# Turning k one slot sooner and q one slot later, and merging the last-key products of a duo, in a fused attention and MLP kernel

## The chip, the cores and the metric

The kernel runs on one core of a Trainium2 chip. The metric is the device time of one execution in microseconds; less is better. A time is the span of the profile plus about 1.8 us (535.75 against 534.0 for the profiled execution of the kernel before).

## The reference

```python
# q, k, v: (8, 8, 576, 64); tau = 0.02
scores = (q @ k.T) / 8
thresh = max(scores, -1) - tau
scores = where(scores >= thresh, scores, -1e9)
attn   = softmax(scores)
x      = (attn @ v)  -> (4608, 512)        # heads side by side
h      = x @ w_in                          # 512 x 2048
out    = (h - tanh(h)) @ w_out             # 2048 x 512
```

## The kernel before

The work is cut into 32 pairs of heads. A pair has nine query tiles of 128 rows, counted j = 0 to 8: four of the first head, one in the middle that holds the 64 rows left over of both heads, four of the second head. The program is a row of slots, one per tile. In a slot TensorE makes the scores of one tile, one step of the MLP of an earlier batch, and the value products of an older tile; a batch of four pairs has 32 MLP steps in 36 slots, so four slots have none. Two neighbouring tiles form a duo, whose ten blocks of transposed weights lie in one tile `pT`; the ninth key block of both tiles (64 keys each) shares one block.

```python
# attend(i): value product of a duo
for ab in range(2):
    blocks = [(4 * ab + ab + c, c) for c in range(4)]
    blocks.append((4, 4 + ab))               # the shared block of weights
    for n, (blk, c) in enumerate(blocks):
        nc.tensor.matmul(out=po[:, (j - 1 - 5 * hh) + ab, :],
            lhsT=pt[:, blk * P : (blk + 1) * P], rhs=vb[:, hh, c, :],
            start=(n == 0), stop=(n == 4))
```

Before a pair's scores, its k and q are split into high and low halves by GpSimd (`split`) and turned (`turn`): by nine TensorE transposes into one of the two big PSUM buffers `ps_big`, which the scores use as well, and a VectorE copy to `kT` or `qT`. GpSimd then copies `kT` to `kS` with the halves swapped. From pair 9, odd pairs' q, and pair 30's, is turned by a transposing transfer instead, which the sync engine's queue issues.

```python
def q_by_dma(p):
    return p >= 2 * HPAIR and (p % 2 == 1 or p == 30)
# ... cut ...
PREP = (
    # ... loads cut ...
    (8, lambda p: split(p, "k")), (7, lambda p: split(p, "q")),
    (5, lambda p: turn(p, "k")), (4, split_v),
)
for p in range(1, NPAIR):
    first = TPP * p - AHEAD                  # slot of the pair's first scores
    for d, f in PREP[3 if p == 1 else 0 :]:
        d -= p == 1 and d in (3, 5)
        plan.setdefault(first - d, []).append(lambda p=p, f=f: f(p))
    d = 5 if q_by_dma(p) else 3 - (p == 1)
    plan.setdefault(first - d, []).append(lambda p=p: turn(p, "q"))
```

## Time and profile before

| | us |
|---|---|
| median of the runs before the change | 537.72 |
| lowest and highest of them | 537.52, 538.24 |
| the profiled run | 535.75 |
| TensorE busy, of a span of 534.0 | 512.9 |
| VectorE, ScalarE, GpSimd busy | 427.2, 438.2, 290.0 |

### The profile page before, as it was taken

The page shows a single profiled execution, that of the slowest core. Times are in us where ns is not written, and L with a number is a line of the kernel's source. Part 1 is how long each engine was busy: PE and PEld are TensorE (multiplying, and loading weights), DVE is VectorE, ACT ScalarE, POOL GpSimd, SP SyncE. Part 2 cuts the span into 40 slices and gives each one's busy share as a digit, 9 for nine tenths or more (in the row PEclk, how much of TensorE's full clock was granted, in tenths as well). Part 3 has the DMA queues.
Part 4 walks back from the last instruction along what each step waited for, and adds up shares of the span by engine and source line. Part 5 has one row for each costly group of instructions (what it writes and reads, how often), then busy time and mean ns, then how long its engine had stood idle before and what let it go on. Part 6 is the DMA issues. An engine that isn't in the chain of part 4 may idle for free.

```text
span 534.0 us, 13042 instructions
## 1 busy us (share of the span) xinstructions
PE 512.9 (96%) x4782; PEld 287.9 (54%) x4782; DVE 427.2 (80%) x1202; ACT 438.2 (82%) x630; POOL 290.0 (54%) x390
## 2 busy tenths in 40 slices
PE   8989899999999999999999999999999999999997
PEld 4666565555555555555555555555555455444444
DVE  5889877989888988889888988898888888554440
ACT  5999888999898989899888989898989989543330
POOL 7999995767555666657555755566665720000000
PEclk9999999999999999999999999999999999999999
DMA  7555656999998888798988999899989985401113
GB/s 209 178 186 147 207 164 146 184 199 181 178 183 178 180 187 196 169 183 188 190 186 183 191 183 185 171 176 196 189 168 187 193 153 107 105 21 39 39 41 79
DMA packets 204768, 85.76 MB, mean 161 GB/s; under 512 B 172320, under 2 KB 197152, under 8 KB 204704
## 3 DMA queue, kind: packets, MB, share of 16 engines
q1 hardware_dynamic: 204112, 84.51, 74.2%
q8 instruction: 37, 0.61, 0.5%
q10 hardware_dynamic: 592, 0.43, 0.3%
q14 instruction: 27, 0.22, 0.1%
HBM read 36.70 MB, written 9.44 MB: 86 GB/s over the span
## 4 chain that ended last, share of the span: by engine, by line
PE 69%; DVE 15%; POOL 7%; ACT 3%; issue 2%; DMA 2%; SPq 0%; DVEq 0%; POOLq 0%; ACTq 0%
PE psY L521 21%; PE psH L495 18%; PE psS L327 14%; DVE sc L337 7%; PE psO L440 5%; DVE g L514 3%; PE psS L317 3%; PE psHt L495 3%; PE ps_k L241 2%; POOL kS L270 2%; DVE kT L264 2%; ACT pT L403 1%; ACT z L374 1%; DVE yo L534 1%; POOL w_in_sb L628 1%
## 5 line engine op out<-in xcount | busy, mean ns | idle before, releaser
L337 DVE TENSOR_SCALAR_CACHE_REDUCE sc<-psS 128x576 f32<-128x576 f32 x288 | 216.1, 752 | 22.4 <-PE psS L327 13.8
L374 ACT ACTIVATE z<-sc,nb 128x576 bf16<-128x576 f32 x256 | 193.4, 768 | 19.7 <-DVE nb L354 19.7
L521 PE MATMUL psY<-w_out_sb,g 128*128 128x512 bf16 (+1 forms) x592 | 146.0, 374 | 0.8 <-DVE yo L534 0.8
L270 POOL COPY kS<-kT 64x1152 f16<-64x1152 f16 x62 | 70.7, 1141 | 127.3 <-DVE nb L354 125.6
L411 ACT ACTIVATE pT<-zT 128x1152 f16<-128x1152 bf16 (+1 forms) x130 | 138.9, 1068 | 0.4 <-DMA zT<-z 0.4
L495 PE MATMUL psH<-xT,w_in_sb 128*128 128x512 bf16 x480 | 124.0, 379 | 2.3 <-DVE g L514 2.3
L327 PE MATMUL psS<-kT,qT 128*128 128x512 f16 (+1 forms) x512 | 104.4, 285 | 6.0 <-DVE sc L337 4.3
L508 ACT ACTIVATE th<-psH 128x512 f32<-128x512 f32 x128 | 75.4, 589 | 36.0 <-PE psH L495 34.8
L327 PEld LDWEIGHTS <-qT 128*128 128x128 f16 x1024 | 72.3, 97 | 55.7 <-issue 8.7
L327 PE MATMUL psS<-kS,qT 128*128 128x512 f16 x496 | 101.3, 286 | 0.8 <-POOL kS L270 0.7
L514 DVE SCALAR_TENSOR_TENSOR g<-th,psH 128x512 bf16<-128x512 f32 x128 | 87.3, 682 | 17.5 <-ACT th L508 17.5
L521 PEld LDWEIGHTS <-g 128*128 128x128 bf16 x592 | 50.7, 98 | 56.9 <-issue 4.0
L495 PEld LDWEIGHTS <-w_in_sb 128*128 128x128 bf16 x576 | 49.2, 98 | 58.2 <-issue 4.5
L440 PEld LDWEIGHTS <-pT 128*128 128x128 f16 x1280 | 55.7, 98 | 25.2 <-issue 1.9
L440 PE MATMUL psO<-vb,pT 128*128 128x65 bf16 x1280 | 61.2, 193 | 0.0
L194 POOL TENSOR_TENSOR khl<-kraw,khl 128x576 f16<-128x576 f32 x31 | 39.7, 1279 | 2.6
L194 POOL TENSOR_TENSOR qhl<-qraw,qhl 128x576 f16<-128x576 f32 x31 | 39.7, 1279 | 2.6
L403 ACT ACTIVATE pT<-psZ 128x640 f16<-128x640 bf16 (+1 forms) x54 | 35.4, 658 | 5.8 <-PE psZ L394 5.4
L264 DVE COPY kT<-ps_k 128x1152 f16<-128x1152 f16 x31 | 23.4, 756 | 14.1 <-PE ps_k L241 14.0
L534 DVE COPY yo<-psY 128x512 f32<-128x512 f32 (+1 forms) x31 | 21.1, 682 | 13.1 <-PE psY L521 11.1
L455 DVE TENSOR_TENSOR osb<-psO,rc 128x256 bf16<-128x256 f32 x64 | 27.2, 424 | 2.2
L354 DVE TENSOR_SCALAR nb<-mx 128x6 f32<-128x6 f32 (+1 forms) x160 | 24.5, 153 | 2.3
(81 smaller groups left out, 508.2 us busy)
## 6 DMA issues: line engine op xcount, KB each, us to landing
vraw<-in_v_dram SPq DMA_DIRECT2D x32, 256.0 KB, 3.8
out_dram<-yo SPq DMA_DIRECT2D x32, 256.0 KB, 2.9
kraw<-in_k_dram SPq DMA_DIRECT2D x31, 256.0 KB, 3.2
qraw<-in_q_dram SPq DMA_DIRECT2D x31, 256.0 KB, 3.7
wt<-in_moe_w_in_dram SPq DMA_DIRECT2D x8, 512.0 KB, 4.5
wt<-in_moe_w_out_dram SPq DMA_DIRECT2D x8, 512.0 KB, 4.5
zT<-z SPq DMA_TRANSPOSE x104, 3.5
kraw<-in_k_dram SPq DMA_DIRECT2D x32, 32.0 KB, 3.0
```

What stands on the lines that cost most here:

```text
L194: nc.gpsimd.tensor_tensor(out=hl[:, :, 1, :], in0=x, in1=hl[:, :, 0, :], op=ALU.subtract)
L270: nc.gpsimd.tensor_copy(out=o, in_=i)
L327: nc.tensor.matmul(out=ps[:, dst], lhsT=lhs, rhs=kk[:, src], start=(n == 0), stop=(n == 1),)
L337: nc.vector.tensor_scalar(out=sc, in0=ps[:, lo : lo + S], scalar1=SC, scalar2=None, op0=ALU.mult, op1=ALU.max, accum_out=mx[:, c : c + 1],)
L374: nc.scalar.activation(out=z, in_=sc, func=ACT.Prelu, bias=nb, scale=1.0, alpha=STEEP)
L403: nc.scalar.activation(out=pt[:, off * P : (off + n) * P], in_=ps[:, 0 : n * P], func=ACT.Exp)
L411: nc.scalar.activation(out=pt[:, 0 : n * P], in_=zts.pop(i)[:, 0:n, :], func=ACT.Exp)
L440: nc.tensor.matmul(out=po[:, (j - 1 - 5 * hh) + ab, :], lhsT=pt[:, blk * P : (blk + 1) * P], rhs=vb[:, hh, c, :], start=(n == 0), stop=(n ...
L495: nc.tensor.matmul(out=ps, lhsT=w_in_sb[:, c, n * P : (n + 1) * P], rhs=xs[m][:, c, :] if m < B else xR[:, c, :, :], start=(c == 0), stop= ...
L508: nc.scalar.activation(out=th, in_=ps, func=ACT.Tanh)
L514: nc.vector.scalar_tensor_tensor(out=gs[m][:, n, :], in0=th, scalar=-1.0, in1=ps, op0=ALU.mult, op1=ALU.add,)
L521: nc.tensor.matmul(out=ps, lhsT=gs[m][:, n, ms * P : (ms + 1) * P], rhs=w_out_sb[:, n, cols], start=(n == 0), stop=(n == DF_C - 1),)
```

## The change

Its intent: one matmul and one weight load less per duo, and turns placed where VectorE's copy does not hold up the reductions.

```diff
-        for ab in range(2):
-            blocks = [(4 * ab + ab + c, c) for c in range(4)]
-            blocks.append((4, 4 + ab))
-            ... ten products of 65 columns, start on the first of five
+        t = j - 1 - 5 * hh
+        nc.tensor.matmul(
+            out=po[:, t : t + 2, :], lhsT=pt[:, 4 * P : 5 * P],
+            rhs=vb[:, hh, 4:6, :], start=True, stop=False, skip_group_check=True,
+        )
+        for n in range(8):
+            ab, c = divmod(n, 4)
+            blk = 5 * ab + c
+            ... eight products of 65 columns, no start
@@
+            if d == 5 and p >= 5:
+                d = 6
@@
-        d = 5 if q_by_dma(p) else 3 - (p == 1)
+        d = 5 if q_by_dma(p) else (2) if p >= 5 else 3 - (p == 1)
```

More of the change, by code (lines that the diff above doesn't have):

```diff
@@ L434, in attend @@
         pt, hh = pts.pop(i), int(j > 4)
-        for ab in range(2):
-            blocks = [(4 * ab + ab + c, c) for c in range(4)]
-            blocks.append((4, 4 + ab))
-            for n, (blk, c) in enumerate(blocks):
-                nc.tensor.matmul(
-                    out=po[:, (j - 1 - 5 * hh) + ab, :],
-                    lhsT=pt[:, blk * P : (blk + 1) * P], rhs=vb[:, hh, c, :],
-                    start=(n == 0), stop=(n == 4),
-                )
+        t = j - 1 - 5 * hh
[6 more added lines that the diff above has]
+            blk = 5 * ab + c
+            nc.tensor.matmul(
+                out=po[:, t + ab, :], lhsT=pt[:, blk * P : (blk + 1) * P],
+                rhs=vb[:, hh, c, :], start=False, stop=(n == 7), skip_group_check=True,
+            )
     osb = {}
```

## The prediction

> **What bounds the kernel now.** I read the page's busy digits first, then the busy time of each engine in equal windows, then the list of waits, and last the order of time around each turn of k and q.
>
> ```profile
> PE   8989899999999999999999999999999999999997
> DVE  5889877989888988889888988898888888554440
> ACT  5999888999898989899888989898989989543330
> ```
>
> TensorE is at nine tenths or more nearly everywhere after the first 60 us; VectorE and ScalarE follow closely until slice 33. "Busy" is no proof for TensorE, because a matmul's record is longer than its turn in the pipe, so I looked at the windows (columns: window, its length, then busy us and count of PE, weight loads, VectorE, ScalarE, GpSimd; clock; DMA share; GB/s):
>
> ```profile
> 60.00:120.00 60.00, 54.56 (x591) 33.88 (x592) 51.62 (x152) 54.19 (x83) 46.14 (x59) 1.00 0.74 172
> 180.00:240.00 60.00, 59.31 (x568) 33.07 (x567) 53.28 (x153) 54.31 (x76) 36.35 (x48) 1.00 0.88 184
> ```
>
> and at the starts in the order of time (start us, us, engine, line, operation, count, wait if any):
>
> ```profile
> 250.91 0.48 PE L440 MATMUL psO<-vb,pT 128*128 128x65 bf16 x10
> 251.22 0.41 PE L327 MATMUL psS<-kT,qT 128*128 128x512 f16 x2
> ...
> 257.75 0.67 PE L241 MATMUL ps_k<-ident_f,khl 128*128 128x128 f16 x9
> 258.25 0.41 PE L327 MATMUL psS<-kT,qT 128*128 128x512 f16 x2
> ...
> 259.61 0.46 PE L429 MATMUL psO<-vb,pT 128*128 128x130 bf16 x5
> 259.90 0.41 PE L327 MATMUL psS<-kT,qT 128*128 128x512 f16 x2
> ```
>
> From start to start, ten value products of 65 columns take 0.31 us (31 ns each; a duo elsewhere takes 0.32), nine 128-column turns 0.50 us (56 ns each), five of 130 columns 0.29 us (58 ns each). The matmuls follow each other at the pace of their columns. In 120 to 420 us TensorE waits visibly for VectorE only 3.7 us in all (2.1 us for scores, 1.6 us for the hidden product); before that there is more. So the kernel is bound by TensorE's columns, and a reordering can win only its waits: little in the steady part, more between 55 and 120 us. The tail after 466 us holds no attention and cannot change.
>
> **What the Trainium skill says.** "TensorE: Matmul & The Clock Gate", section "Back-to-back issue gap", gives N/2.4 + 2.5 ns for a warm matmul: 29.6 ns for 65 columns, 55.8 for 128, 56.7 for 130. The trace agrees within 2 ns. The same section says that in a stream of weight load and matmul pairs 128 columns cost about 81 ns; the trace doesn't: every ps_k turn has its own load and comes 56 ns after the last. So a weight load is hidden here, and dropping one wins nothing by itself. The same page, "Architectural detail: the array is 16× 32×32, not 1× 128×128", says that VectorE's queue is strictly first in, first out. The trace agrees, as the 1.08 us below shows: a copy that waits for its turn holds up the reductions behind it. "PSUM — Partial Sum Buffer", the rule on accumulation, says that a first matmul clears the written bits of the whole bank, so that a second first in the same bank would spoil an open group. The new order has one first per duo, so nothing is spoilt; no run yet shows it.
>
> **The change, part by part.**
>
> *Value product.* There are 4 duos in each of 32 pairs of heads, 128 in all (1280 products of 65 columns now). Each changes from ten 65-column products to one of 130 and eight of 65. By the starts above: before 10 x 31.5 = 315 ns, after 58 + 8 x 31.5 = 310 ns. The columns stay; one matmul's fixed cost and a hidden load go. 128 x 5 ns = 0.6 us, all on TensorE's path. The first product now needs the late half of pT, but TensorE shows no wait for ScalarE at this line today, only 1.9 us of "issue".
>
> *k a slot sooner (27 pairs, from pair 5).* The nine turns move from behind the 64-column scores of the middle tile (L317) to before them. No work is added. What moves is the 0.76 us copy on VectorE:
>
> ```profile
> 229.00 1.04 PE L495 MATMUL psH<-xT,w_in_sb 128*128 128x512 bf16 x4
> 229.88 0.48 PE L440 MATMUL psO<-vb,pT 128*128 128x65 bf16 x10
> 230.20 0.67 PE L241 MATMUL ps_k<-ident_f,khl 128*128 128x128 f16 x9
> ...
> 230.97 0.76 DVE L264 COPY kT<-ps_k 128x1152 f16<-128x1152 f16 x1 [1.08 <-PE ps_k L241]
> ```
>
> VectorE stands 1.08 us at the copy because TensorE does a hidden product (0.87 us) and a duo (0.32 us) first. Over the run such waits are 14.0 us in 21 places. After the change the turn comes just behind the step of the slot before, which has no duo, so much of that idle time goes and the copy's 0.76 us is done before the scores of the next tile arrive. VectorE starts some 0.7 us less late. This is worth something only where lateness reaches TensorE: once in four pairs, where four slots have no MLP step:
>
> ```profile
> 236.97 0.41 PE L327 MATMUL psS<-kT,qT 128*128 128x512 f16 x2 [0.15 <-DVE sc L337]
> 237.21 0.41 PE L327 MATMUL psS<-kS,qT 128*128 128x512 f16 x2
> 237.84 0.41 PE L327 MATMUL psS<-kT,qT 128*128 128x512 f16 x2 [0.22 <-DVE sc L337]
> ```
>
> With the hidden pipe the two stalls are about 0.3 and 0.4 us of pitch. Most of it stays: the scores started at 235.36 end near 236.0, their reduction (0.75 us) began at 236.16, so VectorE can be at most 0.15 us earlier there, and the second reduction follows at once. I count 0.15 us for each of six such places (pairs 9, 13, ... 29): 0.9 us.
>
> *q a slot later (TensorE-turned pairs only).* In the steady part the score behind the q turn loses about 0.12 us in one pair of four; I let it go, 6 x 0.12 = 0.7 us. Between 60 and 92 us it costs more:
>
> ```profile
> 74.63 0.41 PE L327 MATMUL psS<-kT,qT 128*128 128x512 f16 x2 [0.44 <-DVE sc L337]
> 90.53 0.41 PE L327 MATMUL psS<-kT,qT 128*128 128x512 f16 x2 [0.83 <-DVE sc L337]
> ```
>
> There the q turn stands in the one slot in which VectorE has the normalisation of a half pair (0.19 + 0.42 + 0.34 us) as well. Moved on a slot it meets none. Half of 0.44 + 0.83 and of pair 5's 0.40 + 0.38 us around 60 to 61 us may go: 1.0 us.
>
> *What it costs.* In pairs 5 and 6 GpSimd is late with casts. Pair 6's low halves of k begin at 67.39 and take 1.28 us, to 68.67, while the middle scores start at 67.96: the sooner turn must wait some 0.7 us. Pair 5 has 57.48 (56.20 + 1.28) against 56.78: again 0.7 us. Part of that returns as waits that are then shorter; I take half of it, 0.7 us lost.
>
> Sum: 0.6 + 0.9 + 0.7 + 1.0 - 0.7 = 2.5 us. I round to 2.3 us for stalls I haven't seen: 537.7 - 2.3 = 535.4 us.
>
> **Rivals.** First, the weight load is the limit of the value product, and a ninth load less frees a whole pair's 31.5 ns: 128 x 31.5 = 4 us, giving about 533. For it speaks that the products alternate above 29.6 ns; against it the 56 ns turns with a load each and the unchanged column count. Second, the q copy becomes a new wait: it now has one slot until its first scores instead of two. In the steady part a slot is 1.6 us (58 us for 36 slots), and copy plus one reduction take 1.5 us, so that it just fits; if it misses by 0.3 us in each of the 14 pairs, 4 us come back, some 538 to 540 us. Third, the sooner k turn takes one of the two big score buffers before the middle scores, which then wait for the reduction of the tile before (ends 241.05 by 240.30 + 0.75, turn would end at 240.97): near nothing, or 0.2 us in 27 pairs, 5 us at worst. Fourth, everything moved was hidden anyway: only the 0.6 us remain, 537.1 us.
>
> **Range and chances.** The steady waits of TensorE and its early ones together are under ten us, 2% is 10.8 us. To be faster by 2% nearly every wait would have to go; to be slower by 2% each of 27 pairs would have to gain 0.4 us. Neither is likely. The range from 533.3 to 537.5 takes in the weight-load rival and the one in which all was hidden, but not new stalls in every pair.
>
> **What would show it.** Right: the 130-column product takes 58 ns to the next start, duos 310 ns; the wait of kT for ps_k falls well below 14 us; the waits at 74.6 and 90.5 us are gone or halved; 0.15 us less at pairs 9 to 29; TensorE's first wait for khl on GpSimd near 57 and 68 us. Wrong: a new wait of scores for the copy of qT in every even pair, a longer wait of the middle scores (L317) for the reductions, or duos of 285 ns.

## More of the kernel before

The profiled run is 2 us shorter than the median.

The waits of the whole run on transfers of q, which the prediction passed over, read (who waited, for what, us in total, times, longest; PEld is TensorE's weight load):

```profile
PEld L327 <- DMA qT<-qhl: 1.9, 4, 0.9
PE psS L327 <- DMA qT<-qhl: 0.4, 1, 0.4
```

## The result, and the profile after

The changed kernel takes 535.74 us (median of 4, 535.43 to 536.77) beside 537.73 us before. The ratio is 0.9965 with an interval of 0.9948 to 0.9982. Ratios here are the mean time of one kernel's fast runs over that of the other's of the same rounds, so they are not quite the ratio of the medians quoted. The result is correct, so the single start flag per duo spoils nothing here.

The busy row and one of the windows hardly differ, but for the DMA share of the window, 0.97 where it was 0.88; in the other windows it moves both ways (same columns as in the prediction):

```profile
PE   8989799999999999999999999999999899999997
```

```profile
180.00:240.00 60.00, 59.41 (x552) 33.47 (x551) 53.56 (x155) 54.62 (x76) 35.48 (x45) 1.00 0.97 184
```

*The value product.* In the order of time, one duo of the changed kernel (start, us, engine, line, operation):

```profile
250.16 0.22 PE L437 MATMUL psO<-vb,pT 128*128 128x130 bf16 x1
250.22 0.42 PE L444 MATMUL psO<-vb,pT 128*128 128x65 bf16 x8
250.47 0.41 PE L327 MATMUL psS<-kT,qT 128*128 128x512 f16 x2
```

From 250.16 to 250.47 the nine products take 0.31 us, within the display's rounding of the ten. Taken exactly from the starts of all 128 duos, the median is 313 ns against 317 ns; the 130-column product with its own load takes 57 ns.

*The turn of k.* It now stands in front of the middle scores (L317), and the copy follows at once:

```profile
226.92 1.03 PE L524 MATMUL psY<-w_out_sb,g 128*128 128x512 bf16 x4
227.78 0.67 PE L241 MATMUL ps_k<-ident_f,khl 128*128 128x128 f16 x9
228.38 0.44 PE L317 MATMUL psS<-kT,qT 128*64 128x512 f16 x4
```

```profile
228.55 0.76 DVE L264 COPY kT<-ps_k 128x1152 f16<-128x1152 f16 x1
229.23 0.15 DVE L354 TENSOR_SCALAR nb<-mx 128x6 f32<-128x6 f32 x1
229.29 0.75 DVE L337 TENSOR_SCALAR_CACHE_REDUCE sc<-psS 128x576 f32<-128x576 f32 x1
```

Before, the copy of the same pair started at 230.97 after 1.08 us of idling. VectorE's waits for ps_k fall from 14.0 us in 21 places to 6.8 us in 15. What it does for the stall that the prediction looked at:

```profile
236.35 0.41 PE L327 MATMUL psS<-kT,qT 128*128 128x512 f16 x2
236.59 0.41 PE L327 MATMUL psS<-kS,qT 128*128 128x512 f16 x2
237.22 0.41 PE L327 MATMUL psS<-kT,qT 128*128 128x512 f16 x2 [0.22 <-DVE sc L337]
```

The first wait (0.15 us before) is no longer listed; by the starts, TensorE lost 0.31 us there before (from one start to the next, beyond what the work between them takes elsewhere) and loses 0.22 us now. The second loss is unchanged at 0.38 us.

*Between 60 and 92 us.* The waits at 74.63 and 90.53 us are gone: the scores at 74.63 us list no wait, and the q turns of pairs 6 and 7, from their start to the scores behind them, take 0.67 and 0.50 us where they took 1.10 and 1.49 us. A part comes back one pair later: pair 8's takes 1.11 us where it took 0.54.

*GpSimd near 57 us.* This one came as predicted for pair 5:

```profile
57.82 0.68 PE L241 MATMUL ps_k<-ident_f,khl 128*128 128x128 f16 x9 [0.72 <-POOL khl L194]
```

*And what no step of the prediction names.* At pair 30, whose q comes by a transfer, the first scores wait:

```profile
420.54 1.03 PE L524 MATMUL psY<-w_out_sb,g 128*128 128x512 bf16 x4
423.11 0.42 PE L327 MATMUL psS<-kT,qT 128*128 128x512 f16 x2 [1.55 <-DMA qT<-qhl]
```

The trace of before has this wait too, but shorter:

```profile
423.42 0.42 PE L327 MATMUL psS<-kT,qT 128*128 128x512 f16 x2 [0.39 <-DMA qT<-qhl]
```

The transfer is not slow. Its data is ready long before, on GpSimd, but the sync queue issues it late. Before (GpSimd's last instruction on q, then the queue):

```profile
413.67 1.28 POOL L194 TENSOR_TENSOR qhl<-qraw,qhl 128x576 f16<-128x576 f32 x1
...
410.88 3.67 SPq L382 DMA_TRANSPOSE zT<-z  x2
...
417.40 1.52 SPq L382 DMA_TRANSPOSE zT<-z  x1
419.01 0.52 SPq L537 DMA_DIRECT2D out_dram<-yo  x1
419.65 1.31 SPq L253 DMA_TRANSPOSE qT<-qhl  x1
```

After:

```profile
410.45 1.28 POOL L194 TENSOR_TENSOR qhl<-qraw,qhl 128x576 f16<-128x576 f32 x1
...
409.58 4.97 SPq L382 DMA_TRANSPOSE zT<-z  x2
...
419.65 1.35 SPq L253 DMA_TRANSPOSE qT<-qhl  x1
```

GpSimd is 3.2 us sooner, and the queue issues at the same 419.65 us. In both traces it is busy without a pause before that: the second of the two zT issues shown ends at 414.55 us, and four loads, a zT and a store follow, each at most 0.12 us after the last. The changed kernel starts that second zT issue 1.35 us sooner (411.92 us against 413.27), but it takes 2.63 us instead of 1.28; why was not taken apart. TensorE ends the MLP step before pair 30 1.46 us sooner and waits 1.16 us longer. To see the account at a glance, here is the start of a pair's first scores in several traces, and the time from pair 4 to the last matmul. Start-up differs by up to 1.1 us between the traces (pair 4 starts at 51.84 to 52.92 us), which the last column leaves out (it is the fourth number less the first).

| trace (us) | pair 4 | pair 29 | pair 30 | last matmul | pair 4 to last |
|---|---|---|---|---|---|
| before | 52.00 | 409.78 | 423.42 | 529.97 | 477.97 |
| before, again | 51.84 | 410.62 | 424.12 | 530.67 | 478.83 |
| after | 52.25 | 408.43 | 423.11 | 529.62 | 477.37 |
| after, again | 52.20 | 408.36 | 423.28 | 529.78 | 477.58 |

So by the one trace of each, 1.35 us are won by pair 29 and 0.36 us remain at the end, while the medians differ by 2.0 us. The experiments had to explain both numbers.

### The profile page after: what moved, and what is told of

Its sections match the earlier page's. It is cut to its first block, busy times and chain, and to the rows that moved or that the text cites. A ratio compares the mean times of both kernels' runs of the same rounds, so it can differ in the third digit from the quotient of the medians.

```text
span 533.6 us, 12797 instructions
## 1 busy us (share of the span) xinstructions
PE 511.7 (96%) x4654; PEld 289.6 (54%) x4654; DVE 427.5 (80%) x1202; ACT 438.3 (82%) x630; POOL 291.0 (55%) x390
## 4 chain that ended last, share of the span: by engine, by line
PE 76%; DVE 8%; POOL 8%; DMA 2%; issue 2%; ACT 2%; SPq 0%; POOLq 0%; DVEq 0%; ACTq 0%
PE psY L524 23%; PE psH L498 19%; PE psS L327 16%; PE psO L444 4%; DVE sc L337 4%; PE psS L317 3%; PE psHt L498 3%; PE ps_k L241 2%; DMA kraw<-in_k_dram 2%; DVE g L517 2%; POOL kS L270 2%; PE psO L429 1%; POOL w_in_sb L631 1%; POOL khl L194 1%; PE ps_q L241 1%
## 5 line engine op out<-in xcount | busy, mean ns | idle before, releaser
L524 PE MATMUL psY<-w_out_sb,g 128*128 128x512 bf16 (+1 forms) x592 | 146.0, 374 | 0.8 <-DVE yo L537 0.8
L444 PE MATMUL psO<-vb,pT 128*128 128x65 bf16 x1024 | 53.3, 194 | 0.0
L444 PEld LDWEIGHTS <-pT 128*128 128x128 f16 x1024 | 44.3, 98 | 11.1
L437 PE MATMUL psO<-vb,pT 128*128 128x130 bf16 x128 | 28.2, 220 | 0.0
```

The lines of the kernel that those rows point to most:

```text
L444: nc.tensor.matmul(out=po[:, t + ab, :], lhsT=pt[:, blk * P : (blk + 1) * P], rhs=vb[:, hh, c, :], start=False, stop=(n == 7), skip_group_ ...
L524: nc.tensor.matmul(out=ps, lhsT=gs[m][:, n, ms * P : (ms + 1) * P], rhs=w_out_sb[:, n, cols], start=(n == 0), stop=(n == DF_C - 1),)
```

## The experiments

Twelve kernels ran, with five rounds each; all gave correct results. Within a call the runs of the kernel before are shared (medians 537.34, 537.00 and 537.87 us); the first two calls ran on one chip, the third on another. At the start theory A was the prediction's own: only stalls between engines count. Its rivals were that the trace of before was a lucky one (B), that the transfers take the gain back (C), and, for the product, that a load is worth a whole turn.

### before_again: the kernel before, unchanged

> The unchanged kernel, once more, for the noise of times and of traces. Theory A (the gain is the stalls that moved: about 1.7 us of it in the traces, from the product and the shorter waits): ratio 1.000 within 0.1%, and the new trace lies like the first one: start of the first score of pair 29 near 409.8 us, and of pair 30 near 423.4 us. Rival B (the trace of before caught a luckily short run, because it reads 535.75 us while the unprofiled runs read 537.5 to 538.2; the usual run has about 2 us more in waits for transfers): the new trace is 1 to 2.5 us longer, and the excess stands in waits on a transfer, most likely at pair 30's transposed q.

Measured: 536.83 us (536.40 to 537.20), ratio 0.9991 (0.9979 to 1.0004). The trace is 0.7 us longer than the first one at the end. Pair 29 starts at 410.62 us, not at 409.8. The excess stands in transfers, but not at pair 30, which waits only 0.24 us: the first scores of pair 27 wait 0.39 us for q, and there is this from ScalarE:

```profile
ACT pT L411 <- DMA zT<-z: 1.5, 2, 1.1
```

It was 0.4 us in one place in the first trace. That is B in kind, though less than B said (1 to 2.5 us, most likely at pair 30): the kernel before loses a varying amount to transfers, and the first trace was a good draw.

### after_again: the changed kernel, unchanged

> The changed kernel once more. Both theories: ratio 0.9965 within 0.15%. Theory A: pair 29 starts its scores again near 408.4 us, 1.35 us sooner than before; the 1.5 us wait of pair 30's first score for the transfer of its q comes and goes. Rival C (the transfer queue is the second bound, and takes back what TensorE wins): the wait at pair 30 is there again, between 1 and 2 us, and the tail starts only 0.3 to 0.5 us sooner than in the trace of before.

Measured: 535.56 us (534.94 to 535.64), ratio 0.9966 (0.9952 to 0.9979). Pair 29 starts at 408.36 us, and pair 30 waits 1.77 us. This is as C said, so the wait belongs to the changed kernel. (The last matmul starts 0.19 us sooner than in the first trace of before, a little less than C's 0.3.)

### product_only: only the merged value product

```diff
 the kernel before, with attend() of the changed kernel
```

> Only the value product of the change; k and q turn when they did. Theory A: 128 duos x 4 ns (317 ns before, 313 ns after, by the starts in the two traces) = 0.5 us, ratio 0.9990 (0.998 to 1.000). Rival (a dropped weight load is worth a whole 31 ns turn): 4 us, ratio 0.9926. Rival C: 0.5 us at pair 29, less at the end.

Measured: 535.56 us (535.49 to 535.72), ratio 0.9969 (0.9957 to 0.9982). Both expected ratios missed, and C's loss at the end too (0.52 us are still there at the last matmul, counted from pair 4). The product alone gives nearly the whole gain of the median, three times its direct 0.5 us. The trace does show the 0.5 us: pair 29 starts 0.51 us sooner when both are counted from pair 4 (357.27 us against 357.78). The duos are the same length as in the changed kernel. The rest must be in what the trace of before, a good draw, does not have.

### q30_by_pe: pair 30's q turned by TensorE

```diff
 changed kernel, and
-        return p >= 2 * HPAIR and (p % 2 == 1 or p == 30)
+        return p >= 2 * HPAIR and p % 2 == 1
```

> The changed kernel, but pair 30's q is turned by TensorE like that of the other even pairs and no transfer is needed for it. It adds nine turns of 56 ns, 0.5 us of TensorE, and one 0.75 us copy on VectorE. Theory A (the wait at pair 30 is a real stall of up to 1.5 us in the changed kernel): 0.5 to 1.0 us faster than after_again in the traces, and the tail starts 1 us sooner. Rival C (the transfers as a whole are late): the wait moves to the transposed zT of the same tiles and the time is that of after_again or 0.5 us longer.

Measured: 534.32 us (534.04 to 534.64), ratio 0.9946 (0.9933 to 0.9958). It is 1.24 us shorter than after_again, a little more than expected, in spite of nine turns more. The last matmul starts at 528.59 us instead of 529.78. The wait at pair 30 is therefore on the path to the end, and doesn't reappear elsewhere.

### before_sooner_transfer and before_sooner_transfer_2: the transfers of q one slot sooner, nothing else

```diff
 the kernel before, and
-        d = 5 if q_by_dma(p) else 3 - (p == 1)
+        d = 6 if q_by_dma(p) else 3 - (p == 1)
```

> The kernel before, with only the transposing transfers of q (13 pairs) issued one slot sooner; nothing on TensorE changes. Theory D (the kernel before loses 1 to 2 us in most runs because the transposed q of pairs 9, 11, 27 and 30 lands just when its first score wants it; the changed kernel's gain in the median is largely that this happens in fewer pairs): landings 1.0 us or more ahead of the first score in all 13 pairs, 1.2 to 1.8 us faster, ratio 0.9970 (0.9962 to 0.9980). Theory A (only TensorE's and VectorE's stalls count): ratio 0.9990 to 1.0005.

Measured: 536.02 us over the five fast runs (536.20 with the slow one), ratio 0.9983 (0.9971 to 0.9995), which just misses both D's range and A's. One run of six was slow (868.82 us at clock 0.558); the profile fell in it, so that there was no fast trace to read. Again:

> The same as before_sooner_transfer, whose one profile fell into a slow run at clock 0.558. Theory D: again ratio 0.998, and its trace shows no first score of a pair waiting for its q, and lies within 0.3 us of the first trace of before at pair 29 and 0.4 us under it at the end, so that the rest of the 1.6 us between that trace's run (535.75 us) and the usual 537.3 us has another cause, to be seen in the trace. Rival: the waits at pairs 9, 11, 27 or 30 are still there.

Measured: 535.93 us (535.54 to 536.48), ratio 0.9968 (0.9955 to 0.9980), so the two differ by what the noise allows. In the trace q lands at least 1.66 us before its first scores in all 13 pairs, and no wait for qT is left. So waits for q are worth between 0.9 and 1.7 us in the usual run of the kernel before. The expected place of pair 29 (within 0.3 us of the first trace) missed: it is 0.80 us later. It already was 0.43 us later at pair 4, and 0.63 us more are lost between pairs 9 and 10 (0.2 us come back at pair 11), where ScalarE waits for another transfer:

```profile
ACT pT L411 <- DMA zT<-z: 2.0, 3, 1.1
```

### after_sooner_transfer: the changed kernel with the same

```diff
 changed kernel, and
-        d = 5 if q_by_dma(p) else (2) if p >= 5 else 3 - (p == 1)
+        d = 6 if q_by_dma(p) else (2) if p >= 5 else 3 - (p == 1)
```

> The changed kernel with the transfers of q one slot sooner. Theory D: the wait of 1.5 to 1.8 us at pair 30 is gone or halved, 534.3 us, ratio 0.994 (0.9930 to 0.9955), as when TensorE turns pair 30's q. Theory A: 535.6 us, ratio 0.9966. If the transfer queue as such were the bound, the waits would turn up at zT, and the time be that of the changed kernel or worse.

Measured: 533.94 us (533.68 to 534.13), ratio 0.9941 (0.9930 to 0.9953), as theory D said. The place in question:

```profile
420.54 1.03 PE L524 MATMUL psY<-w_out_sb,g 128*128 128x512 bf16 x4
421.40 0.41 PE L327 MATMUL psS<-kT,qT 128*128 128x512 f16 x2
```

The first scores of pair 30 follow the MLP step after its own 0.86 us, with no wait; q landed at 419.48 us. From pair 4 to the last matmul the trace takes 475.64 us, against 477.37 us for the changed kernel.

### k_and_q: only the turns

```diff
 the kernel before, with the two plan lines of the changed kernel
```

> The two turns as in the change, the value product as before. Theory A: everything but the product's 0.5 us, so 1.2 us faster, ratio 0.9975. Theory D: in the trace six gains of about 0.2 us at pairs 9 to 29 less a loss of 0.2 to 0.9 us at pairs 4 and 5, a wait of 0.5 to 1.3 us at pair 30, ratio 0.997 to 1.000. If k and q were worth nothing, as product_only at 0.9969 beside 0.9966 for the whole change suggests, ratio 0.9990 to 1.0010.

Measured: 536.51 us (534.82 to 537.70), ratio 0.9987 (0.9971 to 1.0003). It lies in theory D's range, but A's 0.9975 lies inside its interval and the third theory's range (0.9990 to 1.0010) overlaps it, so the ratio decides nothing. The trace tells more: from pair 13 to pair 29 it takes 231.26 us against 231.89 in the kernel before, so 0.63 us are won there; then

```profile
424.73 0.42 PE L327 MATMUL psS<-kT,qT 128*128 128x512 f16 x2 [1.63 <-DMA qT<-qhl]
```

and from pair 4 to the end it is 0.39 us longer than the first trace of before (478.36 us).

### k_only: only k

```diff
 the kernel before, and
+            if d == 5 and p >= 5:
+                d = 6
```

> k a slot sooner from pair 5, q as before. Theory: loses 0.7 us near 57 us waiting for GpSimd's halves of k (0.9 us at the start of pair 5's scores by the trace of the changed kernel), part of it returned by pair 8; gains 0.09 us at each of pairs 13 to 29. Net between 0 and 0.5 us faster at pair 29, ratio 0.999 to 1.001. Rival (k alone carries the reordering): ratio 0.9975.

Measured: 536.16 us (535.54 to 537.63), ratio 0.9987 (0.9974 to 1.0001). From pair 4 to pair 29 it takes 357.52 us, 0.26 us less than before, as expected, including a 0.51 us wait for q at pair 11. It also corrects an attribution. The prediction gave 0.12 us per four pairs to the later q, for the score behind the q turn. In this kernel q turns where it always did, and:

```profile
246.59 0.67 PE L241 MATMUL ps_q<-ident_f,qhl 128*128 128x128 f16 x9
247.10 0.41 PE L327 MATMUL psS<-kT,qT 128*128 128x512 f16 x2
```

Nine turns take 0.51 us, so nothing is lost there any more (0.62 us before, from 245.92 to 246.54). It is so in all five such places between 120 and 365 us: 0.50 to 0.52 us here, 0.62 in the trace of before. The sooner k alone had removed it; that it did so by leaving VectorE less late fits, but was not shown.

### product_order_only: the new order without the merging

```diff
 product_only, but the first product of a duo split
-        nc.tensor.matmul(out=po[:, t : t + 2, :], lhsT=pt[:, 4 * P : 5 * P],
-            rhs=vb[:, hh, 4:6, :], start=True, ...)
+        for ab in range(2):
+            nc.tensor.matmul(out=po[:, t + ab, :], lhsT=pt[:, 4 * P : 5 * P],
+                rhs=vb[:, hh, 4 + ab, :], start=(ab == 0), ...)
```

> The kernel before with the new order of the value product (shared block of weights first, one first flag per duo), but with ten 65-column products: no matmul and no load is saved. Theory E (the 4 ns per duo that the merged product saves, and the transfers that then land in time by a little, make the gain of product_only): 317 ns per duo as before, ratio 0.9990 to 1.0005. Rival F (the order or the flags do it, not the merging): ratio 0.9970, as product_only.

Measured: 537.44 us (537.09 to 538.14), ratio 0.9997 (0.9984 to 1.0011). Its interval does not touch that of product_only (0.9957 to 0.9982). So it is the merging, not the order or the flags. Its trace has the waits on transfers again:

```profile
ACT pT L411 <- DMA zT<-z: 2.2, 2, 1.7
```

Together with the other traces this gives a pattern. The transfer of q takes, from issue to landing, 5.2 to 5.6 us at pair 11 in the five traces at the old transfer slot that have ten products per duo (before, before_again, k_only, k_and_q, product_order_only), and 5.3 to 5.8 us at pair 27. In the four with the merged product (product_only, after, after_again, q30_by_pe) it takes 4.2 to 4.6 and 3.8 to 4.1 us, and no first score waits there. Nor do these four list any wait of ScalarE for zT.

The traces say more about why. The page lists a DMA queue of kind "instruction" (packets, MB, share); it reads, before and after:

```profile
q8 instruction: 37, 0.61, 0.5%
q8 instruction: 36, 0.59, 0.5%
```

Every kernel with ten products per duo has 37 of these 16 KB packets, every one with nine has 36; it also has 128 matmuls and 128 weight loads less. The traces hold the time of each single packet. In the five traces with ten products one packet starts at 144.1 to 146.0 us, inside the transfer of pair 11's q, and one inside that of pair 27's. In the four it starts at 147.3 to 148.1 us, after pair 11's q has landed, and none falls in pair 27's. At pairs 17 and 19 it is the other way round: there the four have a packet in the transfer, which takes 4.3 to 4.7 us, and the five have none and take 3.2 to 3.9 us; but q lands in time in all nine. In 13 traces, the 47 transfers of q with such a packet starting inside them have a median of 4.5 us, the 121 without one 3.4 us. ScalarE's wait near 124 us follows the packet too (0.4 to 1.7 us, as a transfer of zT lands; in k_only and k_and_q the view puts it down to TensorE). It is there when the packet starts at 119.3 to 120.4 us, during that transfer or just before it, and absent when it starts at 123.9 to 124.7 us. One kernel with nine products, k_from_7_sooner_transfer below, has the packet at 120.4 us, and a wait of 1.1 us with it. So what counts seems to be when the packet comes, and the merging moves it. No run moved the packets alone, so this path is not shown by an experiment.

### product_sooner_transfer: the product and the sooner transfer, old turns

```diff
 product_only, and the transfer line of before_sooner_transfer
```

> The value product of the change and the sooner transfer of q; the turns of k and q on TensorE as before. By the traces the turns are worth 0.85 us at the start of pair 29 (1.35 for the whole change less 0.5 for the product) once no transfer takes it back. Theory: 534.8 us, 0.85 us longer than after_sooner_transfer's 533.94, ratio 0.9958. Rival (the turns of k and q are worth nothing, as 0.9969 beside 0.9966 says): 534.0 us, ratio 0.9941.

Measured: 535.49 us (535.30 to 535.75), ratio 0.9960 (0.9947 to 0.9972), as expected by the ratio. The microseconds are 0.7 above the expected ones, since the kernel before was 0.9 us slower. Against after_sooner_transfer's 0.9941, the turns of k and q are worth about 1 us (0.0019 of 537) when no transfer takes it back. The rival's 0.9941 lies just outside the interval; the two intervals overlap a little (0.9947 to 0.9953), so zero is unlikely rather than excluded by the times. From pair 4 to the last matmul the traces say 1.4 us (477.05 against 475.64).

### k_from_7_sooner_transfer: k sooner only where GpSimd is ready

```diff
 after_sooner_transfer, and
-            if d == 5 and p >= 5:
+            if d == 5 and p >= 7:
```

> The changed kernel with the sooner transfer, and k turned sooner only from pair 7: pairs 5 and 6 don't wait for GpSimd's halves. Theory: the 0.9 us lost at the start of pair 5's scores stays away, of which 0.6 us were already returned by pair 6; so 0.2 to 0.5 us faster than after_sooner_transfer, 533.5 us, ratio 0.9934. Rival (VectorE and ScalarE take back all of it by pair 8): 533.9 us, ratio 0.9941.

Measured: 533.67 us (533.01 to 533.79), ratio 0.9922 (0.9910 to 0.9935). It has the lowest ratio, below both expected ones. The comparison with after_sooner_transfer crosses two calls, in which the kernel before differs by 0.87 us, so its size is uncertain: 0.27 us by the medians, 1.0 us by the ratios. The traces, from pair 4 to the last matmul, differ by 0.26 us (475.38 against 475.64), as expected. They are 0.62 us apart from pair 9 to pair 30, and 0.37 us of that is lost again between pairs 30 and 31, where ScalarE has the longest of these waits:

```profile
ACT pT L411 <- DMA zT<-z: 3.3, 4, 1.3
```

## Why the prediction was right or wrong

The number was right: 535.7 us for 535.4 predicted, inside the range of 533.3 to 537.5 us. That it came so close is in part luck: the sum reached it partly by other terms than its own.

- **The value product, 0.6 us.** Right in mechanism and size: 4 ns per duo, 128 x 4 = 0.5 us. Left out was an indirect part of about 1.2 us: with the merged product the usual run loses less to the transfers of q and zT (product_only 0.9969, order alone 0.9997). That merging does it is shown; the path, by all traces the times of the "instruction" packets, is not tested by itself.
- **k in the steady part, 0.9 us.** The copy's wait fell by half, as said. The gain at the scores in the slots without an MLP step is 0.09 us a place, not 0.15, which fits VectorE's waits for scores (13.8 us before, 19.0 after): part of its lead may have gone into waiting for its input. There are five such places, not six: pair 9 has a single wait, 0.25 us in both traces. But the 0.12 us entered for q also comes from k, so that k wins about 0.21 us in each group of four pairs. Pairs 13 to 29, four such groups, are 0.71 us shorter in k_only (231.89 - 231.18), and 0.87 us shorter in the changed kernel beyond what the product wins there (231.89 - 230.80, less 231.89 - 231.67).
- **q in the steady part, 0.7 us.** This step failed in its attribution: k_only shows that k alone removes the stall behind the q turn. k_only and k_and_q have the same ratio, 0.9987. The places are five here too. Together the two terms were 1.6 us; from pair 9 to pair 29 the changed kernel wins 1.46 us by one trace of each, of which product_only has 0.51, so about 0.95 us are left for k and q.
- **The early part, 1.0 won and 0.7 lost.** The 0.72 us wait of pair 5 came. Pair 6's did not, since TensorE was by then later itself. From pair 4 to pair 9 the net gain is 0.14 us (67.70 us before, 67.56 after) for 0.3 predicted. k_from_7_sooner_transfer, in which k of pairs 5 and 6 turns when it did before, splits it: its 66.93 us are 0.77 us less than before, so the sooner k of these two pairs loses about 0.6 us. Both terms were a little smaller than predicted.
- **Rivals.** The load as the limit (4 us) is out: 313 ns per duo, where it needed 285. A wait for the copy of qT in even pairs did not appear in the steady part; VectorE now waits 7.3 us for ps_q, with no loss on TensorE that the traces show. The middle scores wait for a reduction once more than before, 0.35 us at pair 8. "Hidden anyway" comes nearest to the fate of the turns, but it was not hidden: it was won, and then lost at pair 30.
- **What was missing.** The step "bound by TensorE's columns, and a reordering can win only its waits" left the transfers out of the list of waits. The transfer of pair 30's q, issued at 419.65 us before and after, took back most of the 1.35 us, which q30_by_pe and after_sooner_transfer show by giving 1.2 and 1.7 us. And the median of before was not the trace of before: the 2 us between them were the hint, and by the two runs of before_sooner_transfer 0.9 to 1.7 us of such a gap are waits for q. The two errors nearly cancelled, which was luck.

## What to carry to other kernels

Compare the profiled run's time with the median before reading a trace: if they differ by as much as the gain you look for, the trace does not show what the gain will come from, and several traces are needed. When an engine is made faster, look at each transfer that lands just ahead of its reader, and ask when its queue issues it, not how long it takes: here data lay ready for 5 to 8 us behind other issues in the same queue, and moving the issue one slot was worth 0.5 to 1.7 us (by the ratios, according to what else was changed), about as much as the reordering of the turns. When a change alters how many instructions an engine has, look also at whether other transfers now meet different ones. Credit a part of a change only after it has run alone and with the waits that mask it taken away.

## What the Trainium skill lacked or had wrong

- "TensorE: Matmul & The Clock Gate", section "Back-to-back issue gap", gives about 81 ns per matmul of 128 columns in a stream of load and matmul pairs. Here nine such pairs take 0.50 to 0.51 us, 56 ns each; the 130-column product with its own load takes 57 ns, and two 65-column products with a load each become one for a saving of only 4 ns. The same section's formula for an isolated gap is what holds in the stream.
- "DMA: Bandwidth & Descriptors", section "Issuing engines are not separate DMA queues", calls the time to initiate a DMA on a sequencer "usually small relative to the DMA itself". Here, in the traces of before and after, a transposing issue of q occupies the sync queue for 1.3 to 2.3 us, of a time to landing of 3.3 to 5.4 us, and a finished q waited 4.7 us (before) and 7.9 us (after) from its last GpSimd instruction's end to its issue at pair 30.
- No page that I read says that a data transfer takes longer when a packet of the "instruction" queue falls inside it. Here the transfers of q with one have a median of 4.5 us from issue to landing, those without 3.4 us; at pair 11 it was 5.2 to 5.6 us with one and 4.2 to 4.6 us without, for the same data and nearly the same place in the queue.
